# A decode block with cached attention: V as the weights of P times V in 4 KB runs, the exponent on transposed scores, and one pool of half buffers

## The chip, the cores and the metric

One core of a Trainium2 chip runs the whole program. The metric is the device time of one execution in microseconds; the time given for a kernel is the median of its runs.

## The reference

Four tokens (batch B = 4, one each) pass through two equal layers. A layer is attention over a cached window and a gated feed-forward network, each behind a layer norm and with a residual. Both layers use the same weights and the same cache.

```
attention: q = norm(x) @ wq                        # 16 heads of 256, from D = 448
           k, v = last 2048 rows of k_cache[b, h], v_cache[b, h]    # 8 kv heads, 2 q heads each
           p = softmax(q . k / 16);  o = p @ v     # per batch entry and head
           x = x + concat(o) @ wo
ffn:       x = x + (silu(norm(x) @ w_gate) * (norm(x) @ w_up)) @ w_down      # F = 1792
```
Everything in memory is bf16. K and V of one batch entry and kv head, a pair in what follows, are 1 MB each, and there are 32 pairs, each used in both layers.

## The kernel before

The kernel works through 64 pairs (32 in each layer). `steps()` fixes their order: the first entry's eight heads in layer 0, then entries staggered so that entry t in layer 0 runs beside entry t-1 in layer 1. Of each entry the last five heads of layer 0 stay in SBUF until layer 1 (`KEEP_K`, `KEEP_V`), so 44 of the 64 pairs load K and V. At the end three pairs of entry 2 and then eight of entry 3 run alone, with a norm, the feed-forward network and the projection of q between entry 3's two layers.

Each K and V comes in two DMAs of half a megabyte, issued from SyncE (L609 for K, L626 for V), into one of `NPOOL` = 15 tiles `half`. K is loaded so that a partition holds 16 consecutive keys; a partition's part of a half is one 4 KB run. V is loaded in another order (`"(a q g) d -> q a g d"`), and a partition gets its part of a half in two runs of 2 KB. VectorE turns K by a transpose of 32x32 blocks (L617) from the raw half into a `KT` tile; there are `NKT` = 6 of these, each as large as two halves, and five of them are kept in the steady state. A raw half is free after its transpose, a half of V after its part of P times V.

For one pair the function `pair` issues:

- GpSimd: q of the head, masked into four groups of rows (L641)
- TensorE: scores, 32 matmuls with K as weights (L637), into a PSUM bank S; the 32 columns hold 16 groups of keys for each of two q heads
- VectorE, TensorE, VectorE: the maximum of each row (L646), spread over the partitions by a matmul (L649), then one bias for each of the two heads (L652)
- ScalarE: two exponents, one for each head (L656)
- TensorE: two matmuls, which reorder P (L660, by `permb`) and sum it (L663), into a PSUM bank Y; ScalarE copies P to SBUF as `pT`, each column twice (L666); VectorE finishes the sum (L669) and GpSimd takes its power of -1 (L687)
- TensorE: P times V, 16 matmuls with four columns of P as weights and 256 columns of V moving (L677); the result has its heads in rows that are spread over partitions, with columns of both signs to be combined
- ScalarE and VectorE: an evacuation (L689) and one that combines it with the bank again (L691); TensorE flips it (L697) so that the head's 256 values lie on partitions; VectorE multiplies by the inverse sum (L702)
- TensorE: the projection by wo (L724), once for each step (one pair, or two pairs of the same head)

The order on each engine is not that of the program. Each call of `g.op` or `g.dma` adds a node with an engine, an estimated duration and a rank; `schedule` runs a list of events over them, in which each engine takes, of the nodes that are ready, the one of least rank. That fixes the order of each engine's queue, and `_place_waits` puts in the semaphore waits. A load takes the half that comes free first in the plan (`pool`), and then waits on the chip for that half's last reader. Loads go out strictly by rank: K 2.2 pairs ahead of its pair, V 1.3 behind; the feed-forward weights at 8.4. Work of the norm, the network and the q projection has the rank of 20 pairs earlier (`CROSS`), so it goes ahead of all pairs.

Of the kernel before, what the change touches and what calls it, by code (L numbers as in the profile page):

```python
# [5 lines left out]
ACT = mybir.ActivationFunctionType  # L6
# [7 lines left out]
B = 4  # L14
D = 448
# [10 lines left out]
NKT = 6  # L26
NPOOL = 15
# [15 lines left out]
TRP = 1  # L43
LAND = 1.5
# [29 lines left out]
class Graph:  # L74
# [12 lines left out]
    def op(self, eng, dur, rank, emit, r=(), w=(), bank=(), acc=()):  # L87

        o = Op(len(self.ops), eng, dur, rank, emit)
        self.ops.append(o)  # L90
# [23 lines left out]
    def dma(self, rank, nbytes, emit, sem, r=(), w=(), run=8192, cell=None):  # L114

        o = self.op(SP, 0.05, rank, emit, r=r, w=w)
        o.run = run
        o.nbytes = nbytes
        o.cell = cell
        if cell is None:  # L120
            self._count(o, sem)
        return o
# [7 lines left out]
    def schedule(self, npool):  # L130
# [15 lines left out]
        while n < len(self.ops):  # L146
            best = None
            for e, lst in avail.items():
                if not lst:
                    continue  # L150
                t = max(free[e], min(ready_at[o] for o in lst))
                if e == SP:
                    first = min((o for o in lst if ready_at[o] <= t + 1e-9), key=lambda o: (o.rank, o.i))
                    if first.cell is not None:
                        if not pool:
                            continue
                        t = max(t, min(pool)[0])
                if best is None or t < best[0]:
                    best = (t, e)
            assert best is not None, "the graph does not complete"  # L160
            t, e = best
            o = min((o for o in avail[e] if ready_at[o] <= t + 1e-9), key=lambda o: (o.rank, o.i))
            if o.cell is not None:
# [4 lines left out]
                self._count(o, f"h{slot[1]}")  # L168
# [6 lines left out]
            if o.nbytes:  # L175
                chan = max(chan, t + DSTART) + o.nbytes / 16 * (0.007 / o.run + 1 / 26.6e3)
# [102 lines left out]
def build(nc, A_x, A_k_cache, A_v_cache, A_wq, A_wo, B_x, B_w_gate, B_w_up, B_w_down, out):  # L279
# [3 lines left out]
    with ExitStack() as es:  # L283
# [9 lines left out]
        KT = [sb(f"KT{s}", [128, 16 * DH], BF16) for s in range(NKT)]  # L293
        identb = sb("identb", [128, 128], BF16)
        permb = sb("permb", [128, 128], BF16)
# [5 lines left out]
        onesf, wrow, lomask = small[:, 0:1], small[:, 1:5], small[:, 5:6]  # L301
        expo = small[:, 6 + 2 * NS + 4 * NY:9 + 2 * NS + 4 * NY]
        negm = [small[:, 6 + 2 * i:8 + 2 * i] for i in range(NS)]
# [6 lines left out]
        xio = KT[NKT - 1][:, 0:D]  # L310
        xio_k = tuple(f"kt{NKT - 1}_{hf}_{q}" for hf in range(2) for q in range(TRP))
# [9 lines left out]
        pmax = [sb(f"pmax{s}", [128, 1], BF16) for s in range(NS)]  # L321
        praw = [sb(f"praw{s}", [128, 32], BF16) for s in range(NS)]
        pT = [sb(f"pT{s}", [128, 16, 2, 2], BF16) for s in range(NY)]
        oh = [sb(f"oh{s}", [128, DH], BF16) for s in range(NY)]
        osel = sb("osel", [128, 2], BF16)
# [11 lines left out]
        R0 = -100.0  # L337
        MM = 0.0272
# [27 lines left out]
        g.op(DVE, 0.2, R0, lambda e: e.tensor_copy(  # L366
            permb[:, :].rearrange("p (r l) -> p r l", l=4), identb[:, :].rearrange("p (l r) -> p r l", l=4)),
            r=("identb",), w=("permb",))
# [3 lines left out]
        iv = identb[:, :].rearrange("p (j y n) -> p j y n", j=4, n=2)  # L372
        g.op(DVE, 0.2, R0, lambda e: e.tensor_reduce(
            osel[:, :], iv[:, :, 0:2, :].rearrange("p j y n -> p n j y"), AX.XY, ALU.max, negate=True), r=("identb",),
            w=("osel",))
        g.op(DVE, 0.2, R0, lambda e: e.tensor_reduce(lomask[:, :], iv[:, :, 1, :], AX.XY, ALU.add), r=("identb",),
             w=("lomask",))
        for p_ in range(NY):
            g.op(DVE, 0.27, R0, lambda e, p_=p_: e.memset(Yb[p_][:, 256:512], 0.0), w=(f"y{p_}",), bank=(f"Y{p_}",))
# [215 lines left out]
        kt_free = list(range(NKT))  # L595
        kt_held, v_held = {}, {}
# [3 lines left out]
        def pair(pos, si, side, nside, t, layer, kvh):  # L600
            p_, s_, q_ = pos % NY, pos % NS, pos % NQ
            if layer == 1 and (t, kvh) in kt_held:
                ks = kt_held.pop((t, kvh))
            else:
                ks = kt_free.pop(0)
                ksrc = A_k_cache[t, kvh, s0:s0 + WIN, :].rearrange("(p j) d -> p (j d)", p=128)
                for hf in range(2):
                    cell = []
                    g.dma(pos - KLEAD, 1 << 19, lambda e, cell=cell, hf=hf: e.dma_start(  # L609
                        half[cell[0]][:, :], ksrc[:, 2048 * hf:2048 * hf + 2048]), None, w=(f"k{pos}_{hf}",), run=4096,  # L610
                        cell=cell)
                    for q in range(TRP):
                        def tr(e, cell=cell, hf=hf, q=q):
                            n = 2 // TRP
                            src = half[cell[0]][:, :].bitcast(UINT32).rearrange("p (l k s) -> p l k s", l=2, k=16)
                            dst = KT[ks][:, :].bitcast(UINT32).rearrange("p (k l r) -> p l k r", k=16, l=4)
                            return e.transpose(dst[:, 2 * hf + q * n:2 * hf + q * n + n], src[:, q * n:q * n + n])  # L617
                        o = g.op(DVE, 1.12 / TRP + 0.06, pos, tr, r=(f"k{pos}_{hf}",), w=(f"kt{ks}_{hf}_{q}",))
                    o.rel = (cell,)
# [203 lines left out]
```

## Time and profile before

| what | value |
| --- | --- |
| time, median of 3 runs | 326.23 us (325.0 to 327.39) |
| span of the profiled execution | 322.9 us; its own time is not listed |
| bytes moved | 105.27 MB, mean 326 GB/s |
| busy: TensorE, VectorE, ScalarE, GpSimd | 72%, 60%, 22%, 26% of the span |
| DMA queue: share of 16 engines | 88.0% |

The span runs from the first to the last instruction of the program. Busy time is the union of an engine's instructions; PEld is the loading of weights on TensorE, which overlaps with PE, the matmuls. In the groups of instructions a row names the line, the engine, the operation, the tiles written and read and their shapes, the count, then busy us and mean ns of one, then the idle time just before them and what ended it. In the chain of work that ended last a piece has its start, its length and its name; "by line" gives shares of the stretch asked for. Rows of waits give the total, the number and the longest. The granted TensorE clock is 1.00 throughout.

### The profile page before, as it was taken

The numbers are of one execution on the slowest core, as the hardware profiler recorded it, in microseconds if no ns is written. First come the engines' busy times: TensorE is split into PE (matmuls) and PEld (weight loads), VectorE is DVE, ScalarE is ACT, GpSimd is POOL, SyncE is SP. The second block draws the span as 40 slices with busy tenths as digits, with TensorE's granted clock in tenths as the row PEclk, the third lists the DMA queues.
The fourth block names the chain that finished last, engine by engine and source line by source line (L and its number), as shares of the span: only waits on it lengthen the run. The fifth ranks groups of instructions, "written<-read, shape, count | busy, mean of one in ns | idle before, by whom it ended". The sixth has DMA issues, their size and how long they took to land.

```text
span 322.9 us, 12873 instructions
## 1 busy us (share of the span) xinstructions
PE 232.6 (72%) x5728; PEld 169.7 (53%) x5728; DVE 192.6 (60%) x608; ACT 72.4 (22%) x289; POOL 84.9 (26%) x199
## 2 busy tenths in 40 slices
PE   3654454446588788578796895679787959889875
PEld 2542322234476465366664653567555636686554
DVE  5386555652145778765447787855377874656332
ACT  1112111111022333211231322113223322123310
POOL 3312111112023223240233331313233413134221
DMA  7999999999999999999889999999899999748000
GB/s 277 399 407 392 393 396 397 391 396 397 391 362 308 338 368 346 400 362 309 301 272 373 375 351 405 355 365 339 277 359 377 357 386 391 277 140 305 5 0 5
DMA packets 42327, 105.27 MB, mean 326 GB/s; under 512 B 3096, under 2 KB 7200, under 8 KB 41888
## 3 DMA queue, kind: packets, MB, share of 16 engines
q1 hardware_dynamic: 42272, 104.45, 88.0%
q8 instruction: 45, 0.74, 0.9%
q14 instruction: 10, 0.08, 0.1%
HBM read 104.44 MB, written 0.00 MB: 323 GB/s over the span
## 4 chain that ended last, share of the span: by engine, by line
DMA 38%; PE 34%; DVE 12%; SPq 7%; issue 5%; ACT 2%; POOL 0%; DVEq 0%
DMA half<-in_A_k_cache_dram 20%; DMA half<-in_A_v_cache_dram 12%; PE Y L677 11%; PE S L637 8%; DVE KT L617 6%; DMA wd_sb<-in_B_w_down_dram 5%; PE Z L473 4%; SPq L389 4%; PE A L724 3%; PE Z L514 3%; DVE oh L691 2%; PE Z L542 2%; SPq L609 2%; DVE small L652 2%; SPq L626 1%
## 5 line engine op out<-in xcount | busy, mean ns | idle before, releaser
L617 DVE STREAM_TRANSPOSE KT<-half 128x1024 uint32<-128x1024 uint32 x88 | 108.3, 1233 | 13.3 <-DMA half<-in_A_k_cache_dram 12.9
L637 PE MATMUL S<-qe,KT 128*128 128x8 bf16 x2048 | 64.6, 168 | 22.4 <-DVE KT L617 18.5
L677 PE MATMUL Y<-half,pT 128*4 128x256 bf16 x1024 | 70.0, 403 | 9.6 <-DMA half<-in_A_v_cache_dram 8.7
L637 PEld LDWEIGHTS S<-qe,KT 128*128 128x128 bf16 x2048 | 59.7, 104 | 30.7 <-DVE KT L617 20.8
L687 POOL TENSOR_TENSOR small<-small 128x2 f32<-128x2 f32 x64 | 44.3, 696 | 113.5 <-DVE small L669 103.3
L656 ACT ACTIVATE praw<-S,small 128x16 bf16<-128x16 f32 x128 | 28.7, 279 | 84.6 <-DVE small L652 83.9
L691 DVE SCALAR_TENSOR_TENSOR oh<-oh,small,Y 128x256 bf16<-128x256 bf16 x64 | 30.1, 472 | 23.9 <-ACT oh L689 23.4
L689 ACT ACTIVATE oh<-Y 128x256 bf16<-128x256 f32 x64 | 24.6, 384 | 74.2 <-PE Y L677 74.2
L641 POOL TENSOR_TENSOR qe<-qc,qmask 128x64 bf16<-128x64 bf16 x64 | 18.6, 294 | 71.3 <-PE S L637 52.3
L677 PEld LDWEIGHTS Y<-half,pT 128*4 128x4 bf16 x1024 | 20.0, 94 | 21.8 <-DMA half<-in_A_v_cache_dram 11.5
L646 DVE TRANSPOSE_TENSOR_REDUCE pmax<-S 128x1 bf16<-128x32 f32 x64 | 13.4, 211 | 27.1 <-PE S L637 25.3
L724 PE MATMUL A<-oT,wo_sb 128*128 128x1 bf16 (+1 forms) x688 | 24.8, 166 | 6.4 <-DVE oT L702 6.1
L724 PEld LDWEIGHTS A<-oT,wo_sb 128*128 128x128 bf16 x688 | 22.2, 105 | 10.5 <-DVE oT L702 8.5
L697 PE MATMUL Y<-osel,oh 128*128 128x2 bf16 x128 | 13.3, 173 | 17.4 <-DVE oh L691 17.2
L652 DVE TENSOR_REDUCE small<-S 128x2 f32<-128x128 f32 x64 | 17.4, 282 | 10.4 <-PE S L649 8.3
L666 ACT ACTIVATE pT<-Y 128x64 bf16<-128x64 f32 x64 | 14.1, 222 | 40.7 <-PE Y L663 40.4
L697 PEld LDWEIGHTS Y<-osel,oh 128*128 128x128 bf16 x128 | 8.8, 111 | 27.0 <-DVE oh L691 24.5
L649 PE MATMUL S<-identb,pmax 128*128 128x128 bf16 x64 | 16.6, 284 | 4.5 <-DVE pmax L646 3.6
L473 PE MATMUL Z<-xn,wq_sb 128*128 128x1 bf16 (+1 forms) x480 | 15.6, 165 | 2.6 <-DMA wq_sb<-in_A_wq_dram 1.9
L473 PEld LDWEIGHTS Z<-xn,wq_sb 128*128 128x128 bf16 x480 | 14.3, 104 | 3.4 <-DMA wq_sb<-in_A_wq_dram 2.0
L669 DVE TENSOR_REDUCE small<-Y 128x2 f32<-128x32 f32 x64 | 11.0, 177 | 7.1 <-ACT pT L666 6.8
L440 POOL TENSOR_SCALAR st<-st 128x1 f32<-128x1 f32 x16 | 4.3, 267 | 41.2 <-DVE st L428 40.7
(76 smaller groups left out, 212.0 us busy)
## 6 DMA issues: line engine op xcount, KB each, us to landing
half<-in_A_k_cache_dram SPq DMA_DIRECT2D x88, 512.0 KB, 7.0
half<-in_A_v_cache_dram SPq DMA_DIRECT2D x88, 512.0 KB, 6.7
wo_sb<-in_A_wo_dram SPq DMA_DIRECT2D x8, 448.0 KB, 12.3
wq_sb<-in_A_wq_dram SPq DMA_DIRECT2D x3, 1024.0 KB, 6.9
wd_sb<-in_B_w_down_dram SPq DMA_DIRECT2D x1, 1568.0 KB, 16.3
wg_sb<-in_B_w_gate_dram SPq DMA_DIRECT2D x1, 1344.0 KB, 14.2
wu_sb<-in_B_w_up_dram SPq DMA_DIRECT2D x1, 1344.0 KB, 14.7
wq_sb<-in_A_wq_dram SPq DMA_DIRECT2D x1, 512.0 KB, 10.4
```

The source lines that it names most:

```text
L473: last = e.matmul(o, lhsT=lhsT, rhs=rhs, start=(cc == 0 and hh == 0 and ee == 0), stop=(cc == 3), skip_group_check=True)
L617: return e.transpose(dst[:, 2 * hf + q * n:2 * hf + q * n + n], src[:, q * n:q * n + n])
L637: last = e.matmul(Sb[s_][:, 8 * gg:8 * gg + 8], lhsT=kt[:, gg, ce // 2, ce % 2, :], rhs=qe[q_][:, ce, :, :], start=(gg == 0 and ce == 0), ...
L641: g.op(POOL, 0.25, pos - SLEAD - 1, lambda e: e.tensor_tensor(qe[q_][:, :, :, :], qc[t][:, kvh, :, :].unsqueeze(2).broadcast_to([128, 8, 4 ...
L652: g.op(DVE, 0.2, pos, lambda e: e.tensor_reduce(negm[s_][:, :], Sb[s_][:, 128:256].rearrange("p (k n) -> p n k", n=2), AX.X, ALU.max, nega ...
L656: g.op(SCA, 0.17, pos, lambda e, n=n: e.activation(praw[s_][:, :].rearrange("p (k n) -> p n k", n=2)[:, n, :], Sb[s_][:, 0:32].rearrange(" ...
L677: last = e.matmul(Yb[p_][32 * gg:32 * gg + 4, 256:512], lhsT=pT[p_][:, 4 * gg + 2 * hv + a, :, :].rearrange("p y n -> p (y n)"), rhs=half[ ...
L687: g.op(POOL, 0.25, pos, lambda e: e.tensor_tensor(ri[p_][:, :], rs[p_][:, :], expo[:, 1:3], op=ALU.pow), r=(f"rs{p_}", "expo"), w=(f"ri{p_ ...
L689: g.op(SCA, 0.28, pos, lambda e: e.activation(oh[p_][:, :], Yb[p_][:, 256:512], ACT.Copy), r=(f"y{p_}",), w=(f"oh{p_}",), bank=(f"Y{p_}",))
L691: g.op(DVE, 0.4, pos, lambda e: e.scalar_tensor_tensor(out=oh[p_][:, :], in0=oh[p_][:, :], scalar=lomask[:, 0:1], in1=Yb[p_][:, 256:512], ...
L697: last = e.matmul(Yb[p_][:, 2 * dh:2 * dh + 2], lhsT=oh[p_][:, :].rearrange("p (m e) -> p e m", e=2)[:, dh, :], rhs=osel[:, :], start=Fals ...
L724: last = e.matmul(Av[:, cc, sl], lhsT=wo_sb[:, 4 * kvh + k, c0:c0 + 128], rhs=oT[si % 2][:, k % 2, k // 2, 0:n], start=False, stop=False, ...
```

## The change

V is loaded as K is, 16 consecutive keys to a partition, in runs of 4 KB. In P times V, V becomes the stationary operand: 32 matmuls with a 128x128 block of V as weights and two columns of P moving, and the result comes out with its values on partitions, so the two evacuations and the flip are gone. The scores are transposed by VectorE in 32x32 blocks; then a partition belongs to one q head, one exponent with one bias for each partition does for both, and a matmul adds -1e30 where the column belongs to the other head before the maximum is taken. P is turned back by four matmuls onto 32 partitions each, and the sum is taken from the copied `pT`. The scores are issued in two halves. Raw K, turned K and V share one pool of 27 halves; a transpose takes a half for its output, a score half gives it back unless the head is kept, and a load may not take the last free half (`RESERVE`).

```
-NKT = 6
-NPOOL = 15
+NPOOL = 27
+RESERVE = 1
...
+                spare = len(pool) > (RESERVE if e == SP else 0)
...
-                chan = max(chan, t + DSTART) + o.nbytes / 16 * (0.007 / o.run + 1 / 26.6e3)
+                chan = max(chan, t + DSTART) + o.nbytes / 16 * (0.009 / o.run + 1 / 27.96e3)
...
+                    def tr(e, raw=raw, hf=hf):
+                        src = half[raw[0]][:, :].bitcast(UINT32).rearrange("p (x k s) -> p x k s", x=4, k=8)
+                        dst = half[ks[hf][0]][:, :].bitcast(UINT32).rearrange("p (k x r) -> p k x r", k=8, x=4)
+                        return e.transpose(dst, src)
+                    g.op(DVE, 1.16, pos, tr, r=(f"k{kk}_{hf}",), w=(f"kt{kk}_{hf}",), cell=ks[hf], rel=(raw,))
...
-                vsrc = A_v_cache[t, kvh, s0:s0 + WIN, :].rearrange("(a q g) d -> q a g d", a=4, q=128)
+                    g.dma(pos + VLAG, 1 << 19, lambda e, hv=hv: e.dma_start(
+                        half[vs[hv][0]][:, :], rows(A_v_cache, hv)), None, w=(f"v{kk}_{hv}",), run=4096, cell=vs[hv])
...
+                if hf == 1:
+                    last = e.matmul(Sb[s_][:, 128:256], lhsT=identb[:, :], rhs=pbig[:, :], start=True, stop=False, ...)
...
+            g.op(DVE, 0.12, pos, lambda e: e.transpose(sT[s_][:, :], Sb[s_][:, 0:32]), r=(f"s{s_}",), w=(f"sT{s_}",),
+                 bank=(f"S{s_}",))
             g.op(DVE, 0.2, pos, lambda e: e.tensor_reduce(
-                negm[s_][:, :], Sb[s_][:, 128:256].rearrange("p (k n) -> p n k", n=2), AX.X, ALU.max, negate=True),
+                negm[s_], Sb[s_][:, 128:256], AX.X, ALU.max, negate=True),
...
-            for n in range(2):
-                g.op(SCA, 0.17, pos, lambda e, n=n: e.activation(...ACT.Exp, bias=negm[s_][:, n:n + 1]),
+            g.op(SCA, 0.17, pos, lambda e: e.activation(praw[s_][:, :], sT[s_][:, :], ACT.Exp, bias=negm[s_]),
...
+                for a in range(4):
+                    last = e.matmul(Yb[p_][32 * a:32 * a + 32, 0:32], lhsT=praw[s_][:, :], rhs=rhs[:, a, :, :], ...)
...
+                Yb[p_][:, 32:64], lhsT=onesb[:, :], rhs=pT[p_][:, :, :], start=False, ...),
...
+                for jj in range(8):
+                    u = 4 * (jj // 2) + 2 * hv + jj % 2
+                    for dh in range(2):
+                        last = e.matmul(Yb[p_][:, 64 + 2 * dh:66 + 2 * dh],
+                                        lhsT=half[vs[hv][0]][:, 256 * jj:256 * jj + 256].rearrange("p (m e) -> p e m", e=2)[:, dh, :],
+                                        rhs=pT[p_][:, u, :], start=False, ...)
...
-            g.op(SCA, 0.28, ... oh ...)
-            g.op(DVE, 0.4, ... oh ...)
-            g.op(PE, 0.06, pos, flip, ...)
             g.op(DVE, 0.09, pos, lambda e: e.tensor_tensor(
-                o_[:, :, :, side], Yb[p_][:, 0:4].rearrange("p (d n) -> p d n", n=2),
+                o_[:, :, :, side], Yb[p_][:, 64:68].rearrange("p (d n) -> p d n", n=2),
```

More of the change, by code (lines that the diff above doesn't have):

```diff
@@ L337, in build @@
         R0 = -100.0
+        BIG = 1e30
         MM = 0.0272
@@ L601, in pair @@
             p_, s_, q_ = pos % NY, pos % NS, pos % NQ
[L602 to L619, printed above, removed]
@@ L669, in pair @@
+            for hv in range(2):
+                g.op(PE, 16 * MM, pos, lambda e, hv=hv: pv(e, hv), r=(f"pT{p_}", f"v{vn}_{hv}"), bank=(f"Y{p_}",),
+                     rel=() if keep_v else (vs[hv],), **(dict(acc=(f"y{p_}",)) if hv else dict(w=(f"y{p_}",))))
             g.op(DVE, 0.1, pos, lambda e: e.tensor_reduce(
```

182 lines of the change are left out of this document (87 added, 95 removed).

## The prediction

> **What bounds the kernel now.** I read the page first (shares, the slices, the chain), then the stages, then each stage's chain.
>
> ```profile
> span 322.9 us, 12873 instructions
> PE 232.6 (72%) x5728; PEld 169.7 (53%) x5728; DVE 192.6 (60%) x608; ACT 72.4 (22%) x289; POOL 84.9 (26%) x199
> q1 hardware_dynamic: 42272, 104.45, 88.0%
> DMA 38%; PE 34%; DVE 12%; SPq 7%; issue 5%; ACT 2%; POOL 0%; DVEq 0%
> ```
> No engine is full, and the chain is shared by DMA and TensorE: an average over unlike stages. So the stages come next (columns: stretch, its length, busy time of each engine with instruction counts, TensorE clock, DMA share, GB/s):
>
> ```profile
> 10.00:90.00 80.00, 42.30 (x1025) 29.91 (x1026) 41.51 (x101) 12.22 (x51) 14.66 (x33) 1.00 1.04 395
> 90.00:267.00 177.00, 140.63 (x3476) 101.01 (x3478) 120.99 (x349) 47.05 (x190) 50.53 (x114) 1.00 0.97 349
> 267.00:286.00 19.00, 17.54 (x483) 13.92 (x476) 8.69 (x43) 3.22 (x12) 4.73 (x12) 1.00 0.89 320
> 286.00:312.20 26.20, 22.55 (x562) 16.57 (x559) 13.60 (x49) 8.14 (x33) 8.82 (x19) 1.00 0.31 103
> ```
> To 90 us the DMA engines are full (share 1.04, 395 GB/s) and TensorE is half idle. From 90 to 267 the rate falls to 349 GB/s: 349 x 177 us are 61.8 MB, which at 395 GB/s take 156.5 us, so 20.5 us of the 177 are lost to something else. From 286 DMA is nearly done and TensorE is busy 86% of the time. What the DMA queue waits for, and what the chain of the two later stages is made of:
>
> ```profile
> SPq L609 <- PE Y L677: 25.0, 17, 3.8
> SPq L626 <- PE Y L677: 19.5, 15, 4.0
> by line: DMA half<-in_A_v_cache_dram 22.6%; DMA half<-in_A_k_cache_dram 16.3%; PE Y L677 13.0%; PE S L637 9.8%; issue 7.7%; DVE KT L617 7.4%; PE Z L473 5.9%; DVE oh L691 2.4%; DVE small L652 2.0%; PE A L724 2.0%; ACT praw L656 1.5%; ACT oh
> by line: PE Y L677 29.1%; PE S L637 22.4%; PE A L724 13.1%; DVE oh L691 6.7%; ACT oh L689 4.5%; DVE KT L617 4.4%; DVE small L652 3.8%; issue 3.3%; PE Y L697 3.0%; PE Y L660 2.9%; ACT praw L656 1.7%; PE Y L663 1.4%; DVE pmax L646 1.2%; PE S
> ```
> The third row is 90 to 267, the fourth 286 to 312.2. The load queue mostly waits for P times V (L677) to give a half buffer back: five kept heads hold 10 of the 15 halves, so five are left for raw K and V in flight. In the middle stage the chain goes 39% through transfers; in the last it is TensorE and the hops between engines.
>
> **The change part by part.** Its own time for the profiled execution is not listed; its span is 322.9 us, 3.3 under the median of 326.23, and I carry those 3.3 us unchanged.
>
> *V in 4 KB runs.* The bytes stay, the packets of V halve. K comes in 4 KB runs already, so the trace has both kinds. Two stretches with full DMA engines, the first with K alone, the second with V nearly alone:
>
> ```profile
> 17.00:19.00 2.00, 1.56 (x48) 1.28 (x44) 1.48 (x4) 0.00 (x0) 0.29 (x1) 1.00 1.01 404
> 24.10:25.60 1.50, 0.63 (x14) 0.34 (x10) 1.50 (x4) 0.22 (x1) 0.48 (x2) 1.00 1.01 378
> DMA packets 219, 0.81 MB, mean 404 GB/s; under 512 B 22, under 2 KB 22, under 8 KB 219
> DMA packets 289, 0.57 MB, mean 378 GB/s; under 512 B 15, under 2 KB 15, under 8 KB 289
> half<-in_A_v_cache_dram SPq DMA_DIRECT2D x88, 512.0 KB, 6.7
> ```
> Without the small ones that is 197 packets of 4.1 KB and 274 of 2.1 KB. A half of V (0.524 MB) takes 1.387 us at 378 and 1.298 at 404: 0.089 us less, 7.8 us over 88 halves. It is paid where DMA ends last. By the order of the steps 18 halves land before 90 us (1.6 us, paid in full), 58 between 90 and 267 (5.2 us), 12 later, where the time is set by others (0). In the middle the bounds are 39% of 5.2, 2.0, by the chain's share, and 5.2; I take 3.6. The windows' saving is 6.4% of a half. The Trainium skill (DMA: Bandwidth & Descriptors, section Why small descriptors are slow) puts a fixed cost of about three 32-byte beats on a packet: as an estimate from that page, 67 beats for 2 KB and 131 for 4 KB, 2.2% saved, and 2.7 us over all halves. By it the windows' difference would mostly be something else than the packet; no row tells, so it is a rival below.
>
> *P times V with V as weights; the flip and its two evacuations go.* The rows of what goes and what stays:
>
> ```profile
> L617 DVE STREAM_TRANSPOSE KT<-half 128x1024 uint32<-128x1024 uint32 x88 | 108.3, 1233 | 13.3 <-DMA half<-in_A_k_cache_dram 12.9
> L691 DVE SCALAR_TENSOR_TENSOR oh<-oh,small,Y 128x256 bf16<-128x256 bf16 x64 | 30.1, 472 | 23.9 <-ACT oh L689 23.4
> L689 ACT ACTIVATE oh<-Y 128x256 bf16<-128x256 f32 x64 | 24.6, 384 | 74.2 <-PE Y L677 74.2
> L697 PE MATMUL Y<-osel,oh 128*128 128x2 bf16 x128 | 13.3, 173 | 17.4 <-DVE oh L691 17.2
> L646 DVE TRANSPOSE_TENSOR_REDUCE pmax<-S 128x1 bf16<-128x32 f32 x64 | 13.4, 211 | 27.1 <-PE S L637 25.3
> L652 DVE TENSOR_REDUCE small<-S 128x2 f32<-128x128 f32 x64 | 17.4, 282 | 10.4 <-PE S L649 8.3
> L669 DVE TENSOR_REDUCE small<-Y 128x2 f32<-128x32 f32 x64 | 11.0, 177 | 7.1 <-ACT pT L666 6.8
> L702 DVE TENSOR_TENSOR oT<-Y,small 128x4 bf16<-128x4 f32 x64 | 9.5, 149 | 5.2 <-PE Y L697 5.1
> L663 PE MATMUL Y<-praw,onesb 128*128 128x32 bf16 x64 | 11.9, 188 | 0.4 <-issue 0.4
> L656 ACT ACTIVATE praw<-S,small 128x16 bf16<-128x16 f32 x128 | 28.7, 279 | 84.6 <-DVE small L652 83.9
> L687 POOL TENSOR_TENSOR small<-small 128x2 f32<-128x2 f32 x64 | 44.3, 696 | 113.5 <-DVE small L669 103.3
> 298.19 0.13 PE S L649
> 298.41 0.95 PE Y L677 x16
> ...
> 304.39 0.05 PE Y L660
> 304.44 0.03 PE Y L663
> 304.47 0.83 PE S L637 x32
> ...
> 311.01 0.05 issue
> ```
> The last six are pieces of the chain near the end (start, length). Back to back, 16 matmuls of P times V add 0.95 us, 32 of the scores 0.83. The new P times V has the form of the scores (128x128 weights in every second element, two moving columns where the scores have eight), 32 a pair, so I price it at 0.83: 0.12 less a pair. Gone too are the 0.384 us on ScalarE, the 0.472 on VectorE and the two flips (two of the 0.03 us issue steps of L663 at least, 0.21 when waited for). Added on TensorE: the mask matmul of -1e30 (nearest row L649, 0.13 with its end, and L660, 0.05, with a quarter of the columns; I take 0.09 between them, since nobody waits for it alone), four 32-row turns for the two matmuls of before (0.12 and 0.03 for the sum, against 0.08 now; +0.07). Net: 0.16 added, 0.12 and 0.06 saved. **TensorE's queue is a wash**; what goes is the hop through ScalarE and VectorE.
>
> Instead of that hop the result now waits for the sum: its matmul comes after the copy of pT rather than before (0.188), then L669 on VectorE (0.177), then the power on GpSimd (0.696), with four handovers of some 0.05 (the last row) 1.3 us behind pT. P times V takes 0.83 plus some 0.2 behind pT, so the last product waits about 0.3 us where it waited 1.2 us (0.384 + 0.472 + 0.21 and handovers). If VectorE sits in a transpose (1.233 us) when the sum is ready, that cover is gone and the pair loses up to 1.2 us; and on GpSimd the masked q of later pairs (L641) and the norms' steps stand behind the later power.
>
> *Exponent on transposed scores.* Added: a 32x32-block transpose of 128x32 on VectorE, priced as L646, which reads the same tile transposed: 0.21 us, with L702 (0.149) and L652 (0.282) as bounds. It stands between the maximum and the bias, on the pair's chain. Removed: one of two exponents, up to 0.279. A wash. VectorE in all loses 0.472 and gains 0.21 a pair, and its wait for ScalarE (23.4 us in total) goes, so transposes start sooner.
>
> *One pool of 27.* 15 halves and six turned tiles of two become 27. The order on the load queue stays, since ranks stay. Kept heads hold 20; 7 are left, of which loads may not take the last. A turned K holds its cells from transpose to scores. A pair of the middle stage:
>
> ```profile
> 239.99 1.25 DVE L617 STREAM_TRANSPOSE KT<-half 128x1024 uint32<-128x1024 uint32 x1 [0.40 <-DMA half<-in_A_k_cache_dram]
> 242.72 1.23 DVE L617 STREAM_TRANSPOSE KT<-half 128x1024 uint32<-128x1024 uint32 x1
> 243.48 0.99 PE L637 MATMUL S<-qe,KT 128*128 128x8 bf16 x32
> ```
> The two cells are held 4.2 (the first is released halfway through the scores) and 1.75 us, 5.95 in all; 29 pairs load in 177 us, one in 6.1, so 0.98 cells on the mean are turned K, and 7 - 0.98 - 1 = 5.0 are left to loads: **as many as now**. I cost it at nothing.
>
> New is that a transpose waits for a cell that a P times V or a score gave back, in VectorE's order. Behind it stand the maximum, transpose, bias, sum and product of the pairs in work, and TensorE waits for these. The plan puts a transpose only where a cell is free; if the chip is later than the plan, it blocks. Setup: two constants for five, and no memsets, all before the first K lands. The output row's own tile costs nothing.
>
> *Sum by stage.* To 90: 1.6. 90 to 267: 3.6 for V, and the hop: L691 is 2.4% of 177, 4.2 us, which I take whole (bounds 0, where the next DMA is late instead, and 8, with L689, flips and earlier transposes). 267 to 286: 0.4 for one hop on the way to the last projection. 286 to 312: L691, L689 and L697 are 14.2% of 26.2, 3.7 us, plus 8 x 0.12 for P times V, less 8 x 0.16 added and 0.3 of the new wait at the end, 3.1. After 312 nothing changes. Together 12.9; 326.2 - 12.9 = **313.3, said as 313**.
>
> **The rivals.**
> - *Longer runs and the hop buy nothing in the middle.* For it: 20.5 us there are lost to full buffers, TensorE's queue isn't shortened, and a K transfer may be late in V's place. Against: 39% of that chain are transfers. Left are 1.6, 0.4 and 3.1: 321.
> - *A packet's length is a third of what the windows say.* If two thirds of the step from 378 to 404 GB/s come from what else runs in the two windows (TensorE 0.42 busy in one, 0.78 in the other) rather than from the packet, the 5.2 us of V in the sum become 1.7 and the time 316.8. For it: the windows are 2.0 and 1.5 us short. Against: the engines are full in both, and K's window is the one with the busier TensorE. The Trainium skill's page DMA: Bandwidth & Descriptors, section Why small descriptors are slow, would put it there.
> - *The pool and the freer VectorE recover much of the slack.* For it: VectorE sheds 0.26 us a pair and its waits, and a turned tile no longer idles in its own pool; of 20.5 us lost, 8 more come back: 305. Against: the count of cells above.
> - *Slower: the pool starves the loads.* Five halves at 349 GB/s turn over in 5 x 0.524 MB / 349 GB/s = 7.5 us. If that holds, the rate goes with the cells: at a mean of d the 177 us become 177 x 5/d. Turned K that waits longer for its scores, or a transpose blocked on a cell, lowers d. At 4.66 the loss is 12.9 us and the gain is gone; at 4.5 it is 19.7: 333. Against: fewer cells also shorten the queue in front of each transfer.
> - *It doesn't do what it says*: masks, turns and the later sum cost what the hop saves, and packets only move the waiting to K: within 1%, some 325.
>
> **How the numbers follow.** Forecast, 308 to 316: 0.42. Packets worth a third, 316 to 318: 0.10. Middle gains nothing, 318 to 323: 0.14. More slack recovered, 300 to 308: 0.12. No change: 0.10. Starved: 0.12. About 1% (3.3 us) is what a measurement here tells from no change, so faster 0.78, same 0.10, slower 0.12. The range from 304 to 327 takes in the neighbours and leaves out the starved case and the far end of the gain.
>
> **What would show it.** V's packets halve (88 x 0.524 MB at 2 KB are 22,500); the DMA rate before 90 us rises from 395 to about 402 (V is 30% of its bytes). TensorE busy stays near 230 us and its count rises by 18 matmuls a pair (32 for 16; mask 1, turns and sum 5 for 2, flips 0 for 2). VectorE falls to about 175, ScalarE to about 37. The middle's rate rises above 349 GB/s. The stretch from the last q projection to the last pair shrinks from 26.2 to about 23 us. It is wrong if the rate from 90 to 267 falls below 349 GB/s, if VectorE's transposes wait for P times V, if 32 matmuls of P times V take over 1 us, or if the product waits long for the power.

## The result and the profile after

The changed kernel takes 347.2 us in the median of four runs (340.9 to 350.1) against 326.0 us (325.0 to 327.4): 1.060 times the time of before, with a 95% interval of 1.041 to 1.079. The forecast was 313 us, so it has the wrong sign. A ratio is taken over the undisturbed runs and a median over all of them, and the profiled executions of the changed kernel (350.1 us, span 348.3), e1, e8, e11 and e14 are among their longer ones. (In the diff above, the destination of the turn should read `"p (k x r) -> p x k r"`.)

The page of the changed kernel: span, busy times, the instruction queue of the DMA engines, and the chain by engine. For comparison, the same queue's row of before is the last line.

```profile
span 348.3 us, 15028 instructions
PE 233.4 (67%) x6880; PEld 209.9 (60%) x6880; DVE 176.4 (51%) x604; ACT 41.6 (12%) x161; POOL 85.7 (25%) x199
DMA packets 31071, 105.41 MB, mean 303 GB/s; under 512 B 3096, under 2 KB 7200, under 8 KB 30624
q8 instruction: 54, 0.88, 1.0%
PE 47%; DMA 19%; issue 15%; DVE 10%; SPq 8%; POOL 1%; ACT 0%; DVEq 0%
```
```profile
q8 instruction: 45, 0.74, 0.9%
```
Nearly every count came as forecast: TensorE busy 233.4 us (said to stay near 230), VectorE 176.4 (175), 18 matmuls more a pair (6880 for 5728). And yet the chain's share of TensorE rose from 34% to 47%, and "issue", time in which an engine waited for nothing that the profile shows, from 5% to 15%: 52 us of 348. The stages (length, busy time of PE, PEld, DVE, ACT, POOL with counts, clock, DMA share, GB/s), first after, then before:

```profile
10.00:90.00 80.00, 45.02 (x1193) 37.45 (x1193) 39.62 (x99) 7.53 (x31) 11.73 (x28) 1.00 1.03 401
90.00:180.00 90.00, 63.15 (x1966) 57.93 (x1966) 47.21 (x151) 11.38 (x44) 21.92 (x49) 1.00 0.86 312
180.00:270.00 90.00, 65.86 (x2023) 60.66 (x2020) 53.64 (x172) 12.25 (x49) 26.57 (x60) 1.00 0.90 325
```
```profile
10.00:90.00 80.00, 42.30 (x1025) 29.91 (x1026) 41.51 (x101) 12.22 (x51) 14.66 (x33) 1.00 1.04 395
90.00:180.00 90.00, 71.84 (x1814) 52.61 (x1812) 58.09 (x172) 23.05 (x93) 25.18 (x58) 1.00 0.95 341
180.00:270.00 90.00, 71.65 (x1732) 50.20 (x1736) 64.06 (x183) 24.82 (x100) 26.04 (x58) 1.00 0.98 359
```
To 90 us the rate is up, as forecast. From 90 us on the DMA rate is down, and so is the busy time of VectorE (it has less to do now) and of TensorE itself, by 8.7 and 5.8 us of 90, though TensorE has no less to do. So neither the transfers nor an engine are at their limit there. The waits of TensorE's matmuls show what holds it:

```profile
PE Y L688 <- issue: 15.5, 7, 2.7
PE S L644 <- issue: 10.7, 7, 3.2
PE A L721 <- issue: 6.2, 2, 3.9
```
(Waiting line, what it waited for, us in total, times, longest; "issue" is no wait that the profile shows. In the kernel before, the largest such row of a matmul is 3.0 us.) The stalls hit whatever TensorE has next: scores, P times V, the projection. TensorE's own order of time, with the number of matmuls in each piece and the idle time ahead of it in brackets:

```profile
120.25 0.56 PE L688 MATMUL Y<-pT,half 128*128 128x2 bf16 x15 [1.21 <-issue]
120.68 0.56 PE L721 MATMUL A<-oT,wo_sb 128*128 128x2 bf16 x16
121.10 0.37 PE L658 MATMUL S<-identb,pmax 128*128 128x128 bf16 x2
121.85 0.59 PE L644 MATMUL S<-qe,half 128*128 128x8 bf16 x16 [0.38 <-DVE small L663]
122.37 0.22 PE L672 MATMUL Y<-identb,praw 128*32 128x32 bf16 x4
122.52 0.59 PE L644 MATMUL S<-qe,half 128*128 128x8 bf16 x16
122.97 0.27 PE L648 MATMUL S<-pbig,identb 128*128 128x128 bf16 x1
123.03 0.23 PE L679 MATMUL Y<-pT,onesb 128*128 128x32 bf16 x1
123.10 0.99 PE L688 MATMUL Y<-pT,half 128*128 128x2 bf16 x32
124.02 0.22 PE L672 MATMUL Y<-identb,praw 128*32 128x32 bf16 x4
124.18 0.72 PE L644 MATMUL S<-qe,half 128*128 128x8 bf16 x21
128.09 0.46 PE L644 MATMUL S<-qe,half 128*128 128x8 bf16 x11 [3.20 <-issue]
```
Count from the stall of 1.21 us to the next of 3.20: 15 + 16 + 2 + 16 + 4 + 16 + 1 + 1 + 32 + 4 + 21 = 128 matmuls. The scores stop in the middle, after 21 of 32. A stall, in what follows, is idle time of over 0.3 us before a matmul that has no wait of its own. All 23 stalls of this trace, 42.9 us in all, lie a multiple of 128 matmuls apart (the last by one less), that is 256 instructions with their weight loads; before there were 7 of them, with 7.6 us. Where TensorE's queue holds more waits, these take places in the block too: counted with them, all 191 stalls of the 18 traces of this case lie at the same place of 256 instructions, give or take one. The row of q8 fits: 0.88 MB in 54 packets is 16 KB a packet, 6880 / 128 is 53.75, and 5728 / 128 is 44.75 for the 45 packets of before. TensorE's program itself comes through the DMA engines, one packet for 128 matmuls, a block in what follows. The stall of 3.85 us before 266.55 (it began at 262.70), in two windows of the DMA view:

```profile
266.55 0.40 PE L721 MATMUL A<-oT,wo_sb 128*128 128x2 bf16 x9 [3.85 <-issue]
```
```profile
DMA packets 121, 0.43 MB, mean 334 GB/s; under 512 B 15, under 2 KB 15, under 8 KB 121
q1 hardware_dynamic: 121, 0.43, 105.1%
```
```profile
DMA packets 97, 0.36 MB, mean 331 GB/s; under 512 B 11, under 2 KB 11, under 8 KB 96
q1 hardware_dynamic: 96, 0.35, 92.1%
q8 instruction: 1, 0.02, 5.0%
```
From 262.7 to 264.0 the engines move K and V alone; the packet with TensorE's instructions is in the window 264.0 to 265.1. Laid packet by packet against the matmuls, the trace shows a rule: the packet of the next block starts after TensorE has entered the block ahead of it, 0.3 to 0.6 us later where DMA is idle (from 324 us on), but 3.45 us later in the median (0.9 to 5.9) from 90 to 290 us; and in all blocks of that stretch that began over 0.3 us late, TensorE went on 2.2 to 2.5 us after their packet had started. So a block takes some 3.45 + 2.35 = 5.8 us in the median there; those that came late took 4.3 to 8.1. TensorE gets through 32 small matmuls in 0.83 to 0.95 us (the chain's pieces) and so through 128 in less than 4.

### The profile page after: what moved, and what is told of

It reads as the page before. It is cut to its first block, busy times and chain, and to the rows that moved or that the text cites. A ratio compares the mean times of both kernels' runs of the same rounds, so it can differ in the third digit from the quotient of the medians.

```text
span 348.3 us, 15028 instructions
## 1 busy us (share of the span) xinstructions
PE 233.4 (67%) x6880; PEld 209.9 (60%) x6880; DVE 176.4 (51%) x604; ACT 41.6 (12%) x161; POOL 85.7 (25%) x199
## 2 busy tenths in 40 slices
DMA packets 31071, 105.41 MB, mean 303 GB/s; under 512 B 3096, under 2 KB 7200, under 8 KB 30624
## 4 chain that ended last, share of the span: by engine, by line
PE 47%; DMA 19%; issue 15%; DVE 10%; SPq 8%; POOL 1%; ACT 0%; DVEq 0%
PE S L644 14%; PE Y L688 12%; DMA half<-in_A_v_cache_dram 10%; DMA half<-in_A_k_cache_dram 9%; DVE half L624 6%; PE A L721 4%; PE Z L517 4%; PE Z L476 4%; SPq L618 4%; SPq L392 2%; SPq L631 2%; PE Y L672 2%; PE S L648 2%; PE Z L545 1%; PE Z L425 1%
## 5 line engine op out<-in xcount | busy, mean ns | idle before, releaser
L624 DVE STREAM_TRANSPOSE half<-half 128x1024 uint32<-128x1024 uint32 x88 | 108.8, 1237 | 25.5 <-DMA half<-in_A_k_cache_dram 15.3
L644 PE MATMUL S<-qe,half 128*128 128x8 bf16 x2048 | 73.3, 169 | 29.5 <-DVE half L624 11.5
L644 PEld LDWEIGHTS S<-qe,half 128*128 128x128 bf16 x2048 | 64.6, 105 | 37.3 <-DVE half L624 13.8
L688 PE MATMUL Y<-pT,half 128*128 128x2 bf16 x2048 | 69.2, 165 | 24.6 <-issue 15.5
L688 PEld LDWEIGHTS Y<-pT,half 128*128 128x128 bf16 x2048 | 64.1, 105 | 28.1 <-issue 16.1
L666 ACT ACTIVATE praw<-sT,small 128x32 bf16<-128x32 f32 x64 | 20.2, 322 | 143.1 <-DVE small L663 143.0
L648 PE MATMUL S<-pbig,identb 128*128 128x128 bf16 x64 | 17.1, 268 | 0.0
L672 PE MATMUL Y<-identb,praw 128*32 128x32 bf16 x256 | 14.3, 208 | 4.2 <-issue 2.4
L679 PE MATMUL Y<-pT,onesb 128*128 128x32 bf16 x64 | 13.6, 214 | 4.2 <-ACT pT L676 4.1
L663 DVE TENSOR_REDUCE small<-S 128x1 f32<-128x128 f32 x64 | 16.0, 251 | 0.0
L701 DVE TENSOR_TENSOR oT<-Y,small 128x4 bf16<-128x4 f32 x64 | 9.5, 149 | 11.3 <-POOL small L698 11.0
## 6 DMA issues: line engine op xcount, KB each, us to landing
wu_sb<-in_B_w_up_dram SPq DMA_DIRECT2D x1, 1344.0 KB, 16.2
```

Of the source, the lines that this page charges most:

```text
L624: return e.transpose(dst, src)
L644: last = e.matmul(Sb[s_][:, 16 * hf + 8 * gg:16 * hf + 8 * gg + 8], lhsT=kt[:, gg, ce // 2, ce % 2, :], rhs=qe[q_][:, ce, :, :], start=(hf ...
L648: last = e.matmul(Sb[s_][:, 128:256], lhsT=identb[:, :], rhs=pbig[:, :], start=True, stop=False, skip_group_check=True)
L663: g.op(DVE, 0.2, pos, lambda e: e.tensor_reduce(negm[s_], Sb[s_][:, 128:256], AX.X, ALU.max, negate=True), r=(f"m{s_}",), w=(f"negm{s_}",) ...
L666: g.op(SCA, 0.17, pos, lambda e: e.activation(praw[s_][:, :], sT[s_][:, :], ACT.Exp, bias=negm[s_]), r=(f"sT{s_}", f"negm{s_}"), w=(f"praw ...
L672: last = e.matmul(Yb[p_][32 * a:32 * a + 32, 0:32], lhsT=praw[s_][:, :], rhs=rhs[:, a, :, :], start=True, stop=True, skip_group_check=True)
```

## The experiments

Theory A: the instructions of the matmuls that were added arrive too late. Theory B, the rival that was on record: the pool starves the loads.

**One part alone: more matmuls without any new work (e1_pv_split).** The kernel before, with each matmul of P times V cut in two:
```diff
-    rhs=half[vs[hv][0]][:, 1024 * a + 256 * gg:1024 * a + 256 * gg + 256], ...
+    for c in range(2):
+        o = 1024 * a + 256 * gg + 128 * c
+        ... rhs=half[vs[hv][0]][:, o:o + 128], ...
```


> The kernel before, with each matmul of P times V (256 columns) issued as two of 128 columns: the same arithmetic and order, the same columns to stream, 16 more matmuls a pair (6752 in all against 5728; the changed kernel has 6880). Theory A (instruction supply: TensorE stops each time 128 matmuls are used up and the next 16 KB of its instructions come late behind the K and V traffic): 336 to 346 us, with stalls of 1 to 3 us that nothing in the profile explains, spaced 128 matmuls. Theory B (the shared pool of halves starves the loads or blocks the transposes): no pool here, 326 us within 1%.

342.3 us, 1.037 [1.025, 1.049]. The chain by engine:
```profile
PE 38%; DMA 31%; DVE 12%; issue 10%; SPq 6%; ACT 2%; POOL 0%; DVEq 0%
PE 233.9 (68%) x6752; PEld 195.2 (57%) x6752; DVE 193.2 (56%) x608; ACT 72.6 (21%) x289; POOL 84.7 (25%) x199
```
TensorE's busy time (232.6 before) hardly moves, its waits without a cause double, to 10% of the chain, and the stalls grow from 7.6 to 22.3 us. The time grows by 16 us (12 by the ratio), with no part of the change in the kernel.

**V in 4 KB runs alone (e2_v_4kb).** The kernel before with V loaded as K is; its probabilities then don't belong to V's keys, so only the time is read.
```diff
-    vsrc = A_v_cache[t, kvh, s0:s0 + WIN, :].rearrange("(a q g) d -> q a g d", a=4, q=128)
+    vsrc = A_v_cache[t, kvh, s0:s0 + WIN, :].rearrange("(p j) d -> p (j d)", p=128)
```

> The kernel before with V read in 4 KB runs and nothing else changed (keys and probabilities no longer match, so the output is not the reference's). My prediction's price of this part alone: 5.2 us saved, 321 us, and some 404 GB/s instead of 395 before 90 us. If the packet matters a third as much: 324. Theory A as such says nothing on it, unless longer packets delay the instruction fetches: then 326 or above, with more stalls than before at the same matmul numbers.

324.6 us, 0.993 [0.988, 0.998].
```profile
10.00:90.00 80.00, 43.20 (x1051) 30.75 (x1051) 42.40 (x104) 12.74 (x53) 14.68 (x33) 1.00 1.03 402
90.00:180.00 90.00, 71.82 (x1817) 52.64 (x1817) 58.08 (x171) 22.91 (x92) 25.34 (x58) 1.00 0.94 340
```
The forecast's price for this part would have given 321. The rate to 90 us is the 402 GB/s of the forecast; from 90 us on it is what it was (341). That half buffers come back no sooner there would explain it, and isn't shown.

**The pool alone, then with 4 KB runs (e4_pool_alone, e6_pool_v_4kb).** The kernel before with 27 cells, raw and turned K in them, the scores split by halves, and the changed kernel's figures for the loads in the plan; e6 loads V in 4 KB runs as well. Scores and V have different orders of keys there, so only the time is read. From e4 to e6:
```diff
-    half[vs[hv][0]][:, :].rearrange("p (a g d) -> p a g d", a=2, g=4), A_v_cache[...].rearrange("(a q g) d -> q a g d", ...)..., run=2048
+    half[vs[hv][0]][:, :], rows(A_v_cache, hv)), ..., run=4096
```

> The pool of 27 halves, the split scores and the new layout of turned K, on top of the kernel before in everything else: V in 2 KB runs, two exponents from PSUM, P as weights (the key order of K and V no longer match, so the output is not the reference's). 53 matmuls a pair, as before. Theory A: 324 to 329 us. Theory B: 338 or more, with the load queue waiting longer in total than before.

> e4 with V in 4 KB runs as well (keys do not match, output not the reference's). If the two gains add: 318 to 319.5 us. If with the pool the loads are the bound again, more of the V part is cashed: 315 to 317. If TensorE is the bound in the middle: 320, as e4.

320.1 us, 0.980 [0.973, 0.987], and 315.4 us, 0.971 [0.966, 0.976]. The stretch from 90 to 270 us, of the kernel before, e4 and e6:
```profile
90.00:270.00 180.00, 143.50 (x3543) 102.80 (x3545) 122.15 (x354) 47.86 (x193) 51.22 (x115) 1.00 0.97 350
90.00:270.00 180.00, 148.95 (x3688) 107.68 (x3689) 124.10 (x368) 49.06 (x197) 52.73 (x120) 1.00 0.99 362
90.00:270.00 180.00, 152.75 (x3782) 110.46 (x3779) 126.20 (x377) 50.08 (x199) 53.56 (x120) 1.00 0.98 371
```
Theory B falls, and e4 is faster than theory A had it too: the pool feeds the loads better (362 GB/s for 350), and long runs, which bring nothing there alone (348 in e2), now add another 9.

**P as the weights again (e3_p_weights), and that with one maximum for both heads (e10_p_weights_one_max).** The changed kernel with the 256-column matmuls, the hop through ScalarE and VectorE and the flips put back; e10 also leaves the mask matmul (L648) out:
```diff
-    if hf == 1:
-        last = e.matmul(Sb[s_][:, 128:256], lhsT=identb[:, :], rhs=pbig[:, :], start=True, stop=False, ...)
```

> The changed kernel with P as the weights again: 16 matmuls of 256 columns, the two evacuations and the flip back; pool of 27, V in 4 KB runs, transposed exponent, mask and turns stay. 57 matmuls a pair, 5984 in all. Theory A: most of the stalls go, 318 to 328 us. Theory B: the pool is the same, 341 or more.

> P as the weights again (as in the run of 331 us) and one maximum for both heads of a pair, so that the mask matmul over 128 columns goes too: 5920 matmuls. If that matmul is what the transposed exponent costs, 322-327 us. If it is the turn and the later sum that cost, within 1% of 331 us.

331.4 us, 1.007 [1.001, 1.013], and 327.3 us, 1.006 [1.001, 1.010]. e3 is over the 328 that theory A allowed. The intervals overlap, so the mask's price isn't settled by time. The busy rows of e6, e3 and e10:
```profile
PE 234.9 (75%) x5728; PEld 171.5 (55%) x5728; DVE 192.4 (61%) x608; ACT 73.2 (23%) x289; POOL 84.8 (27%) x199
```
```profile
PE 254.2 (77%) x5984; PEld 183.0 (56%) x5984; DVE 202.4 (62%) x673; ACT 66.2 (20%) x225; POOL 85.5 (26%) x199
```
```profile
PE 247.1 (76%) x5920; PEld 179.3 (55%) x5920; DVE 202.0 (62%) x673; ACT 66.2 (20%) x225; POOL 85.7 (26%) x199
```
From e6 to e3 only the exponent's side changes, and TensorE is busy 19.3 us more: 0.30 us a pair, of which the mask is 7.1 / 64 = 0.11. That stands beside 16 us of time (12 by the ratios), while the stalls grow by 3.8 us only, from 7.4 to 11.2: the larger part of it is not the supply.

**V as the weights alone (e11_v_weights_alone).** e6 with the changed kernel's product and without the hop; e6's keys, its exponent without mask and turn, and the pool stay.
```diff
-    last = e.matmul(Yb[p_][32 * gg:32 * gg + 4, 256:512], lhsT=pT[p_][:, u, :, :]..., rhs=half[vs[hv][0]][:, 256 * jj:256 * jj + 256], ...)
+    for dh in range(2):
+        last = e.matmul(Yb[p_][:, 64 + 2 * dh:66 + 2 * dh], lhsT=half[vs[hv][0]]...[:, dh, :], rhs=pT[p_][:, u, 0, :], ...)
```

> The pool, V in 4 KB runs and V as the weights, with the exponent as it was before: no mask, no turn, and neither the eviction of the product nor the two turning matmuls. The probabilities do not belong to V's keys, so only the time is read. Against the run of 315.4 us (pool and 4 KB) it takes the hop of L691, L689 and L697 away and puts 32 matmuls of 128 x 2 in place of 16 of 256 columns and 2 small ones. By the prediction's sum (the hop 4 to 7 us, matmuls a wash): 308-312 us. Theory A: 14 more matmuls a pair, in a stretch that is dense with small ones, put stalls without a wait on the path again and eat the gain: 322-334 us, with 15 us or more of such stalls.

332.4 us, 1.021 [1.010, 1.033]; e6 is at 0.971.
```profile
PE 216.8 (65%) x6624; PEld 197.5 (59%) x6624; DVE 170.2 (51%) x544; ACT 50.2 (15%) x225; POOL 84.9 (25%) x199
PE 39%; DMA 27%; issue 14%; SPq 10%; DVE 7%; ACT 2%; DVEq 0%
```
This is the cleanest case against the forecast's sum: TensorE has 18 us, VectorE 22 us and ScalarE 23 us less to do than in e6, no handover is added, and the program takes 17 us longer (16 by the ratios). Only the matmuls are more, 6624 for 5728, and the stalls grow from 7.4 to 37.1 us.

**The changed kernel with fewer matmuls (e5_fewer, then e9_time_equal).** Sixteen products of V in place of 32, each with the columns of P repeated, 128 in e5 and 52 in e9; half of V's columns take no part:
```diff
-    for dh in range(2):
-        last = e.matmul(Yb[p_][:, 64 + 2 * dh:66 + 2 * dh], lhsT=...[:, dh, :], rhs=pT[p_][:, u, :], ...)
+    last = e.matmul(Yb[p_][:, 64:116]..., lhsT=...[:, jj % 2, :],
+                    rhs=pT[p_][:, u, :].unsqueeze(1).broadcast_to([128, 26, 2]), ...)
```


> The changed kernel with the 32 matmuls of P times V of a pair replaced by 16 of 128 moving columns (P's two columns repeated 64 times) over half of V's blocks: about the same time on TensorE, weights of the same kind, 1024 matmuls fewer (5856). It leaves out half of V, so its output is not the reference's. Theory A (instruction supply): about 20 us less than the changed kernel, 320 to 332 us, the unexplained stalls mostly gone. Theory B' (the longer chain of a pair, mask, transpose, turns, late sum, costs the time): 338 us or more.

346.2 us, 1.065 [1.058, 1.072]: the time is a miss. The stand-in was too dear; TensorE became the bound:
```profile
PE 281.9 (82%) x5856; PEld 257.6 (75%) x5856; DVE 176.2 (52%) x604; ACT 41.6 (12%) x161; POOL 85.5 (25%) x199
L687 PE MATMUL Y<-pT,half 128*128 128x128 bf16 x1024 | 125.0, 310 | 6.5 <-DMA half<-in_A_v_cache_dram 5.7
PE Y L687 <- issue: 0.7, 1, 0.7
```
The 1024 products take 125.0 us of it, 122 ns each, where about 53 would have been a fair exchange. But of the stalls 1.2 us are left, as theory A has it for a TensorE that takes longer over each block.

> The changed kernel with each pair's 32 products of V (2 moving columns each) replaced by 16 of 52 moving columns; half of V's columns take no part in the result. From the run of 128 columns (122 ns each, about a column a ns) 52 columns should take about 52 to 55 ns, twice what a small one takes, so that TensorE's own time stays within some 5 us of the changed kernel's 233 us, while it has 1024 matmuls less (5856, half an instruction block a pair less). Theory A (TensorE's instructions arrive too late): stalls without a wait fall from some 43 us to under 15 us and the time to 318-330 us. Rival (the order of the work or the pool costs it, not the number of instructions): within 1.5% of the changed kernel, 338-348 us.

316.4 us, 0.977 [0.970, 0.984].
```profile
PE 223.8 (71%) x5856; PEld 197.9 (63%) x5856; DVE 175.3 (55%) x604; ACT 41.6 (13%) x161; POOL 85.7 (27%) x199
PE 36%; DMA 33%; DVE 12%; SPq 9%; issue 8%; POOL 1%; ACT 0%; DVEq 0%
90.00:180.00 90.00, 72.15 (x1974) 65.14 (x1972) 56.91 (x183) 14.11 (x55) 27.65 (x62) 1.00 0.96 365
```
Pool, order, mask, turns, late sum and power are those of the changed kernel; 1024 matmuls less, 9.6 us less TensorE time, and 31 us come back (27 by the ratios). The stalls fall by 26.7 us, to 16.2, a little above the 15 that were expected (the time is a little under its 318), and the rate in the second stage rises from 312 to 365 GB/s.

**One maximum for both heads in the changed kernel (e8_one_maximum).** 64 matmuls less: the mask is left out as in e10.

> The changed kernel without the mask matmul: the maximum is taken over both heads of a pair, which shifts both exponents alike, and the result is the reference's. 64 matmuls fewer (6816) and 0.05 to 0.13 us of TensorE a pair. Theory A: half an instruction block and 3 to 8 us of TensorE time, 335 to 343 us. If the mask is hidden behind the scores: no change.

338.5 us, 1.040 [1.033, 1.047], with 39.7 us of stalls: 64 matmuls are half a block in 53.75, and the interval lies within that of the changed kernel.

**Why a block is late (e12_half_the_bytes, e13_three_in_flight).** e12 loads the first half of each half buffer's columns only, with the same instructions, and sets the rest once; there are as many packets as in the changed kernel (31071), those of K and V half as long. e13 makes each load of a half wait until the third before it has landed (it counts bytes; as every such load has half a megabyte, that comes to the lines shown).
```diff
-    half[raw[0]][:, :], rows(A_k_cache, hf)), None, ...          # e12; V alike
+    half[raw[0]][:, 0:1024], rows(A_k_cache, hf)[:, 0:1024]), None, ...
+    loads = [o for o in order[SP] if o.cell is not None]         # e13
+    for i in range(3, len(loads)):
+        loads[i].deps[loads[i - 3]] = True
```

> The changed kernel with every load of K and V cut to the first half of the columns (the rest of each half buffer is set once); same instructions in the same order, about half the traffic. The time will be lower anyhow, so the stalls of TensorE without a wait are what is read. Theory A1 (the blocks of TensorE's instructions wait behind the data on the DMA engines): with those half idle the stalls fall from some 43 us to under 15 us, although TensorE gets through a block sooner. Theory A2 (a block takes its microseconds whatever the traffic): 30 us or more of stalls remain, the time is 290-325 us.

> The changed kernel with one more wait on each load of a half: it is issued when the third load of a half before it has landed, so at most 1.5 MB of K and V are under way where about 5 loads (7.4 us from issue to landing) are now. Everything else, the order on every engine too, stays. Theory A1 (a block of TensorE's instructions waits behind the K and V packets queued on the same DMA engines): the lag of a block shrinks to about 3 loads' time (4 us), stalls without a wait fall from 43 us to under 28 us and the time to 320-335 us. Rival (the depth of the queue does not matter to a block): stalls stay at 35 us or more, and the time is the changed kernel's or longer, 341-355 us, since loads start later.

e12: 306.6 us, and stalls of 11.0 us, although TensorE is busier in the second stage (76.5 us of 90, for 63.2 in the changed kernel) and so through with a block sooner:
```profile
90.00:180.00 90.00, 76.51 (x2388) 70.65 (x2385) 60.01 (x191) 14.38 (x56) 28.62 (x63) 1.00 0.60 192
PE 63%; DVE 20%; POOL 9%; issue 7%; ACT 0%; DVEq 0%; POOLq 0%
```
With 192 GB/s on the engines a packet starts 1.6 us after TensorE enters a block, for 3.45. e13: 392.0 us, 1.197 [1.178, 1.217]; the time was a miss for both theories.
```profile
DMA 85%; PE 8%; SPq 4%; DVE 2%; issue 1%; POOL 0%; ACT 0%; DVEq 0%
half<-in_A_k_cache_dram SPq DMA_DIRECT2D x88, 512.0 KB, 5.8
10.00:90.00 80.00, 35.90 (x944) 29.31 (x945) 36.08 (x75) 6.73 (x28) 8.26 (x19) 1.00 0.89 310
```
```profile
10.00:90.00 80.00, 31.10 (x815) 25.38 (x815) 31.34 (x66) 6.21 (x26) 7.27 (x17) 1.00 0.77 263
```
With three loads under way (two in the last row, of e14) a load of K still takes 5.8 us to land (7.5 in the changed kernel), so the engines aren't filled: 310 GB/s to 90 us for 401. The packets' lag shrinks to 2.7 us and the stalls to 14.9, but TensorE waits for data then. Lag goes with traffic in both runs, which is what queueing behind K and V looks like; which rule orders the packets, no run shows.

**The same depth elsewhere (e14 to e16).** Two in flight in the changed kernel; three in e7, below; three in the kernel before.

> As the run with three loads of a half under way, with two (1 MB, some 2.6 us at 400 GB/s). Theory A1: stalls fall further, to under 18 us, but the rate before 90 us falls under 400 GB/s because a load's way from issue to first packet is no longer covered; in all 318-340 us. Rival: stalls as in the changed kernel, and 345-370 us.

> The pool with two half-size turns a half, V in 2 KB runs and P as weights (322.8 us before, 9.5 us of stalls without a wait), with at most three loads of a half under way. Theory A1: a few us of the 9.5 us go, 316-322 us. Rival: no change or a loss, 322-330 us.

> The kernel before with at most three loads of a half under way; nothing else changes. It has 7.6 us of stalls without a wait. Theory A1: 320-326 us. Rival (loads that start later cost more than the blocks gain): 327-335 us.

462.8, 368.6 and 367.6 us (1.419, 1.134, 1.130): misses too, for the reason that e13 shows.

**The pool without the rest (e7_pool_two_turns).** The pool with V in 2 KB runs, P as weights and the exponent as before; each raw half is turned in two parts, so that scores and V have the same keys and the whole reference is computed.

> The pool of e4 with matching keys, so that it computes the reference: each raw half of K is turned by two transposes of half the size into two cells, two cells are kept back, V in 2 KB runs, everything after the scores as before. Two more fixed costs of VectorE a pair (some 0.15 us each) and a turned cell is held for longer. Theory A has nothing against it: 320 to 324 us, faster than before by 1 to 2%. If the pool's gain hangs on the half-wise release of turned K: 325 or more.

322.8 us, 0.994 [0.990, 0.998]: a little faster than the kernel before, and the fastest of the runs that leave nothing of the computation out; no run that computes all of it gains more than these 0.6%.

## Why the prediction was wrong, point by point

By the medians, 326 us become 320 with the pool (e4), 315 with long runs of V (e6), 331 with the exponent on transposed scores (e3) and 347 with V as weights. So the pool and the long runs gained some 11 us, and the two other parts lost 12 to 17 each, by ratios and medians.

- **The step that failed: "TensorE's queue is a wash".** In busy time it is (232.6 to 233.4). The forecast had the 18 matmuls more a pair among its own signs, but priced a matmul by its duration alone and its supply at nothing. Supply costs a packet each 128 matmuls, and a block takes some 5.8 us in the median beside K and V at 312 to 325 GB/s, where TensorE is through with 128 small matmuls in less than 4. Going by span, 35 us more of stalls stand against 25 us of lengthening. That sum is no proof, since a stall can lie beside other waits; e11, with no other part changed, is, and so is e9. That the busy time is a wash is luck in part, since the 0.30 us a pair that was added and the 0.33 that was saved were priced at 0.16 and 0.18 (below). So is it that e9's 316.4 us lie near the forecast's 313, since they hold a gain of the pool that stood at nothing in the sum.
- **The second step that failed: the exponent on transposed scores, "a wash".** Masks, turns and later sum, priced at 0.16 us a pair on TensorE, measured 0.30: the mask 0.11 for 0.09, the turns and the sum 0.19 for 0.07. Five matmuls of 32 columns don't cost their issue steps alone. The sum charges them for the last 8 pairs and sets them off elsewhere against what P times V saves. In e3 this and the longer way from maximum to P cost 16 us together (12 by the ratios); they weren't told apart, and the cause stays open. Beside V as weights the price is much the same, 347.2 for the 332.4 of e11 (13 us by the ratios). It need not cost that much: e9 has all of these parts, with 1024 matmuls less, and takes 316.4.
- **P times V** at 0.83 us for 32 was right (the chain has 0.83 for 32 of them), and V as weights saved TensorE 254.2 - 233.4 = 20.8 us, 0.33 a pair for 0.18. It paid with packets.
- **V in 4 KB runs**, 5.2 us in the sum. The 1.6 us before 90 us hold (e2, 402 GB/s). In the middle they buy nothing alone; with the pool it is 4.8 us by the medians (320.1 to 315.4) and 3.0 by the ratios, whose intervals overlap, so the time doesn't decide between the two prices. The packets do: in the kernel before, from 14 to 90 us, 4769 packets of 2 KB took 87.5 ns in the mean and 2855 of 4 KB 163.8 ns, 6.4% less for the same bytes. That is the windows' price, and what went wrong in the middle is how much of it reaches the time. The 2.2%, or 2.7 us over all halves, worked out as an estimate from the Trainium skill (DMA: Bandwidth & Descriptors, section Why small descriptors are slow), is less than these packets show.
- **The pool**, "as many as now", costed at nothing, gained 2%. The count of mean cells was too coarse (the first turned cell of the pair shown is held 4.0 us, not 4.2, which alone changes little). Starved loads were the only rival on the slower side: the right sign, with a mechanism that e4 refutes. The rate fell below 349 GB/s from 90 us on, which the prediction named as a sign of error, but because TensorE gave cells back late: K's and V's loads wait 151 us in all for TensorE, for 126 in e9, most of all in this row.

```profile
SPq L618 <- PE S L644: 32.0, 10, 7.0
```
- **The hop** in the last stretch was to bring 3.1 us. From the last of q's selection matmuls (L491, L494) to the last product (L702, L701) it is 24.5 us before, 26.7 after with a stall of 2.67 in it, 23.3 in e9: a gain of 1.2.
- **VectorE** at 175 was right (176.4); **ScalarE** at 37 was 41.6. **The wait for the power**, 0.3 us, is 0.4 on the mean of the 27 pairs that have it:

```profile
DVE oT L701 <- POOL small L698: 11.0, 27, 0.8
```

The Trainium skill (Runtime: NRT & Kernel Launch, section Instruction fetch mechanics) describes this very supply, blocks of 16 KiB with 256 instructions over a DMA queue of their own, and calls the cost of a block's border mostly hidden. The trace agrees on the block (16 KB, 128 matmuls with their loads); on the cost it doesn't, with up to 3.9 us a border and 42.9 us in all.

## What to carry to other kernels

Count an engine's instructions as traffic: where it issues small ones densely (here 128 matmuls in 4 us) while the DMA engines are full, price the blocks, not only the durations, and prefer one wide matmul to two narrow ones of the same time (e1, e9). When "issue" grows on the chain, count instructions between the stalls; an even spacing that ignores the code's structure (256 instructions in all 18 traces here) points to the supply. And test a rewrite of several parts in parts: here two of four gained.

## What the runs showed of the hardware that was not expected

- A packet of instructions starts 0.3 to 0.6 us after TensorE enters the block ahead when DMA is idle, and 3.45 us in the median (up to 5.9) at 312 to 325 GB/s; TensorE goes on 2.2 to 2.5 us after the start.
- Less work on TensorE, VectorE and ScalarE made a kernel slower (e11: 216.8 us of TensorE, 332.4 us of time; e6: 234.9 and 315.4).
- Three loads of half a megabyte under way give 310 GB/s to 90 us and two 263, where an uncapped queue gives 401.
- For the same bytes, packets of 4 KB took 6.4% less DMA time than packets of 2 KB (163.8 ns for twice 87.5, in the kernel before to 90 us).
